# Decode attention, forward and backward: the K and V loads of the forward given to the load queue in the order in which their buffers come free

## The chip, the cores and the metric

The kernel runs on one core of a Trainium2 chip. The metric is the device time of one execution in microseconds (us), as a median of several executions. All runs told here were fast; executions of one kernel lie within about 0.5% of its median. A ratio of two kernels is the mean time of the fast runs of one over the mean of the other's in the same rounds, so it is not quite the ratio of the medians quoted.

Engines: PE is TensorE, DVE is VectorE, ACT is ScalarE, POOL is GpSimd, SP is the queue that issues the loads of K, V and the weights.

## The reference, cut to what matters

```python
def _A_ref(x, k_cache, v_cache, wq, wo):        # Sq = 1, 32 heads, Sk = 8192, Dh = 192, bf16
    q = (x @ wq) ...
    scores = einsum('bhqd,bhkd->bhqk', q, k) * Dh ** (-0.5)
    p = softmax(scores)
    o = einsum('bhqk,bhkd->bhqd', p, v)
    return o.reshape(...) @ wo
# around it: layer norms, an adaptive modulation and a small MLP.
# The result is the output and the gradients of nine inputs, among them k_cache and v_cache.
```

Each head has 3.1 MB of K and 3.1 MB of V. The forward reads both once, and along the way collects per-head matrices from K and the weighted V that spare the backward a second pass over K. The backward reads V once more and writes dK and dV.

## The kernel before

The forward is a software pipeline over heads. In the pass i of the loop, head i gets its scores (`x`), head i-1 its softmax and three of four quarters of the matmuls with K and weighted V (`y`), and head i-2 the last quarter and its output (`z`). K lies in five buffers of 1.57 MB (half a head each), V in three.

```python
NKB = 5                                       # K buffers, used in turn
vp = ctx.enter_context(tc.tile_pool(name="vp", bufs=3))   # V buffers
# ...
def load_k(h, t):
    kb = KB[(2 * h + t) % NKB]
    nc.sync.dma_start(out=kb, in_=K_hd[h][:, t * JH : (t + 1) * JH, :])
    return kb
# ...
ORDER = {mybir.EngineType.PE, mybir.EngineType.DVE, mybir.EngineType.Activation}
# ...
with tc.manual_schedule(engines=ORDER):       # these engines: as written; SP is left to the scheduler
    for i in range(HQ + 2):
        # ...
        if x is not None:
            x["k"] = [load_k(i, 0), load_k(i, 1)]
            x["v"] = [load_v(i, 0)]
            # ...
        if y is not None:
            dot_sum(y["d1"], y["S"][:, JH:J])              # DVE
            # ...
        if x is not None:
            pa = dot_mul(x["k"][0], qh)                    # DVE, first product of the head (line 264)
        # ...
        if z is not None:
            m_quarter(3, z["k"][1], ...)                   # PE; frees K buffer of (i-2, 1)
        # ... softmax of head i-1 on ACT ...
        if x is not None:
            dot_half(pa)                                   # DVE
            x["d0"] = dot_tree(pa, psR, DH // 2)           # PE, six matmuls 128x512 (line 275)
        if y is not None:
            vs0 = scale_v(0, y["v"][0], E4, Ef)            # 9 of 16 rows on DVE, 7 on ACT (line 319)
            m_quarter(0, y["k"][0], vs0, ...)
            vs1 = scale_v(1, y["v"][0], E4, Ef)            # frees V buffer of (i-1, 0)
        if x is not None:
            x["v"].append(load_v(i, 1))
        if z is not None:
            mt = m_out(...)                                # ACT, three copies from PSUM
        if last:                                           # odd i
            po = pair_sums(...)                            # PE, one-column f32 matmuls
        # ...
            m_quarter(1, y["k"][0], vs1, ...)              # frees K buffer of (i-1, 0)
        # ... second product, pair_o on DVE, third quarter, weight loads ...
        if y is not None:
            y["vs"] = scale_v(3, y["v"][1], E4, Ef)        # frees V buffer of (i-1, 1)
```

The queue's order was whatever the scheduler made of this. In the built program it repeats every two heads; with even h: V(h,1), weights, **K(h+1,0)**, K(h+1,1), V(h+1,0), K(h+2,0), V(h+1,1), K(h+2,1), V(h+2,0) (the load of the output weights moves a little).

Of the kernel before, what the change touches and what calls it, by code (L numbers as in the profile page):

```python
# [20 lines left out]
def kernel(  # L21
# [29 lines left out]
    _, HQ, S, DH = A_k_cache.shape  # L51
# [59 lines left out]
    def tcol(n, name, dtype=FP32):  # L111
        return tmp.tile([P, n], dtype, name=name)
# [67 lines left out]
    def load_w(view3, lo, hi):  # L180
        w = wst.tile([P, ND, CW], BF16, name="w_st", tag="w", bufs=1)
        nc.sync.dma_start(out=w[:, :, 0 : hi - lo], in_=view3[:, :, lo:hi])
        return w

    def load_wo(t):

        w = wst.tile([P, 3, D], BF16, name="wo_st", tag="wo")
        nc.sync.dma_start(out=w, in_=wo_v[t])
        return w
# [67 lines left out]
    def load_v(h, t):  # L257
        v = vp.tile([P, JH, DH], BF16, name="v_sb")
        nc.sync.dma_start(out=v, in_=V_hd[h][:, t * JH : (t + 1) * JH, :])
        return v  # L260

    def dot_mul(src, vec):
        prod = pp.tile([P, JH, DH], BF16, name="prod", tag="prod")
        V_.tensor_tensor(out=prod, in0=src, in1=vec[:, None, :].to_broadcast([P, JH, DH]), op=ALU.mult)  # L264
        return prod
# [12 lines left out]
    def dot_sum(ps, dst):  # L278
        V_.reduce_sum(out=dst, in_=ps, axis=AX.X)  # L279
# [5 lines left out]
    with tc.tile_pool(name="kp", bufs=1) as kp, tc.tile_pool(name="vs", bufs=3) as vsp, tc.tile_pool(name="ft", bufs=2) as ft, \  # L285
# [7 lines left out]
# [4 lines that stand above are left out]
# [9 lines left out]
        def scale_v(q, v, E4, Ef):  # L306
            vs = vsp.tile([P, JQ, VW], BF16, name="vs")
            j0 = q * JQ
            v0 = (q % 2) * JQ
            n = JQ - NVA  # L310
            A_.copy(out=vs[:, :, DH:VW], in_=E4[:, j0 : j0 + JQ, :])
            V_.tensor_tensor(  # L312
                out=vs[:, 0:n, 0:DH].rearrange("p j (a b) -> p j a b", b=4),
                in0=v[:, v0 : v0 + n, :].rearrange("p j (a b) -> p j a b", b=4),
                in1=E4[:, j0 : j0 + n, None, :].to_broadcast([P, n, DH // 4, 4]),
                op=ALU.mult,
            )
            for k in range(n, JQ):
                A_.activation(out=vs[:, k, 0:DH], in_=v[:, v0 + k, :], func=ACT.Copy, scale=Ef[:, j0 + k : j0 + k + 1])  # L319
            return vs  # L320

        def m_quarter(q, kb, vs, mp, op):
            j0 = (q % 2) * JQ
            z = q == 3
            for k in range(JQ):
                T_.matmul(mp[:, 0:MW], lhsT=kb[:, j0 + k, 0:P], rhs=vs[:, k, 0:MW], start=(q == 0 and k == 0), stop=(z and k == JQ - 1), skip_group_check=True)  # L326

            for k in range(JQ):
                p0 = 64 * (k % 2)
                T_.matmul(mp[p0 : p0 + 64, MO : MO + MW], lhsT=kb[:, j0 + k, P:DH], rhs=vs[:, k, 0:MW], start=False, stop=(z and k >= JQ - 2), skip_group_check=True)  # L330

            for k in range(JQ):
                p0 = 32 * (k % 4)
                T_.matmul(op[p0 : p0 + 32, 0:MW], lhsT=ones_bf, rhs=vs[:, k, 0:MW], start=(q == 0 and k < 4), stop=(z and k >= JQ - 4), skip_group_check=True)  # L334
# [49 lines left out]



        ORDER = {mybir.EngineType.PE, mybir.EngineType.DVE, mybir.EngineType.Activation}
        w = load_w(wq_v, 0, CW)
        for b in range(2):
            q_half(0, b, w)  # L390
        mb = MB0
        X, os_, wo_l = {}, {}, {}
        wch = None
        with tc.manual_schedule(engines=ORDER):
            for i in range(HQ + 2):
                x = X[i] = {} if i < HQ else None
                y = X.get(i - 1) if 0 < i <= HQ else None
                z = X.pop(i - 2) if i > 1 else None
                last = z is not None and i % 2 == 1
                t = (i - 3) // 2  # L400
                if x is not None:
                    x["k"] = [load_k(i, 0), load_k(i, 1)]
                    x["v"] = [load_v(i, 0)]
                    x["S"] = ft.tile([P, J], FP32, name="S_h")
                    qh = qs_bc[:, i * DH : (i + 1) * DH]
                    if i % 2 == 0:
                        wo_l[i // 2] = load_wo(i // 2)
                if y is not None:
                    dot_sum(y["d1"], y["S"][:, JH:J])
                    m1 = tcol(1, "m1")  # L410
                    V_.reduce_max(out=m1, in_=y["S"], axis=AX.X)
                if x is not None:
                    pa = dot_mul(x["k"][0], qh)
                if y is not None:
                    mx = psB.tile([P, P], FP32, name="mx", tag="b")
                    T_.matmul(mx, lhsT=m1[:, 0:1].to_broadcast([P, P]), rhs=ident_f, start=True, stop=True)
                if z is not None:
                    m_quarter(3, z["k"][1], z["vs"], z["mp"], z["op"])
                if y is not None:
                    negm = tcol(1, "negm")  # L420
                    V_.reduce_max(out=negm, in_=mx, axis=AX.X, negate=True)  # L421
                    E4, Ef = softmax(i - 1, y["S"], negm)
                if x is not None:
                    dot_half(pa)
                    x["d0"] = dot_tree(pa, psR, DH // 2)
                if y is not None:
                    y["mp"] = psM.tile([P, 512], FP32, name="mp")
                    y["op"] = psO.tile([P, 256], FP32, name="op")
                    vs0 = scale_v(0, y["v"][0], E4, Ef)
                    m_quarter(0, y["k"][0], vs0, y["mp"], y["op"])  # L430
                    vs1 = scale_v(1, y["v"][0], E4, Ef)
# [3 lines that stand above are left out]
                    mt = m_out(i - 2, z["mp"], z["op"], os_)  # L435
                if last:
                    po = pair_sums((os_.pop(i - 3), os_.pop(i - 2)))
                if i % 4 == 3 and wch is not None:
                    q_half((i + 1) // 4, 0, wch)
                if y is not None:  # L440
                    m_quarter(1, y["k"][0], vs1, y["mp"], y["op"])
                if x is not None:
                    pb = dot_mul(x["k"][1], qh)
                if z is not None:
                    m_add(i - 2, z["mp"], mt)
                if last:
                    o2 = pair_o(t, po)
                if x is not None:
                    dot_half(pb)
                    x["d1"] = dot_tree(pb, psR, DH // 2)  # L450
                if y is not None:
                    vs = scale_v(2, y["v"][1], E4, Ef)
                if last:
                    A_.copy(out=AO[:, :, 2 * t : 2 * t + 2], in_=pair_ao(o2, wo_l.pop(t)))
                    e_rows_out(t, e_rows(t))
                if i % 4 == 3 and wch is not None:
                    q_half((i + 1) // 4, 1, wch)
                    wch = None
                if i % 4 == 1 and wch is not None:
                    mod_blocks(mb, nb, wch)  # L460
                    mb += nb
                    wch = None
                if i % 4 == 2 and i + 2 < HQ:
                    wch = load_w(wq_v, ((i + 2) // 4) * CW, ((i + 2) // 4 + 1) * CW)
                if i % 4 == 0 and mb < NMB:
                    nb = min(CW // P, NMB - mb)
                    wch = load_w(wm_v, mb * P, (mb + nb) * P)
                if y is not None:
                    m_quarter(2, y["k"][1], vs, y["mp"], y["op"])
                if x is not None:  # L470
                    dot_sum(x["d0"], x["S"][:, 0:JH])
                if y is not None:
                    y["vs"] = scale_v(3, y["v"][1], E4, Ef)
            while mb < NMB:
                nb = min(CW // P, NMB - mb)
                mod_blocks(mb, nb, load_w(wm_v, mb * P, (mb + nb) * P))
                mb += nb
# [126 lines left out]
    with tc.tile_pool(name="bk1", bufs=1) as bk1, tc.tile_pool(name="ob", bufs=4) as ob, tc.tile_pool(name="bst", bufs=1) as bst:  # L604
# [149 lines left out]
        for t in range(NT):  # L754
            k = max(0, (27 * t) // 8 - 2)
# [15 lines left out]
        for h in range(HQ):  # L771
            doh = do_bc[:, h * DH : (h + 1) * DH]
            qh = qs_bc[:, h * DH : (h + 1) * DH]
            for t in range(2):
                js = slice(t * JH, (t + 1) * JH)
                v = load_v(h, t)
# [54 lines left out]
```

## Time and profile before

| | before |
|---|---|
| median (first 3 runs) | 1650.76 us |
| first product of the last head in the forward | 674.2 us after the start |
| the rest (middle, backward) | 972.7 us |
| time from head to head, heads 3 to 31 | 21.43 us on average |
| DVE's wait for K, line 264 | 102.7 us |

These are lines of the profile page of the kernel before: busy time and share by engine; 40 slices of 41 us, with PE's busy tenths, the clock granted to PE in tenths, DMA's busy tenths and the traffic; and the group of DVE's products with K (after the bar: busy time and mean; then the idle time before them, and what ended most of it).

```profile
PE 1240.7 (75%) x11811; PEld 665.2 (40%) x11811; DVE 1107.8 (67%) x1273; ACT 895.8 (54%) x1948; POOL 108.3 (7%) x193
...
PE   3778887878787878865684878887678878788764
...
PEclk7898988989898988875567655567565555555555
DMA  9988878878787878754989999999999999999988
GB/s 384 366 319 304 321 299 325 329 295 334 311 326 310 347 296 329 280 214 170 380 349 399 370 401 388 403 416 422 414 386 403 389 395 376 365 394 404 405 341 330
...
L264 DVE TENSOR_TENSOR prod<-KB,qs_bc 128x6144 bf16<-128x6144 bf16 x64 | 214.7, 3355 | 120.2 <-DMA KB<-in_A_k_cache_dram 102.7
```

The forward fills the first 17 slices. There no engine is full, not even the fullest, DMA, at a share of 0.84 and 321 GB/s, and yet the largest named wait is for K data. The next line gives the stretch from 64 to 500 us, which is all forward: start and end, length, then busy time of PE, PE weight loads, DVE, ACT, POOL, and last PE's granted clock, DMA's busy share and GB/s.

```profile
64.00:500.00 436.00, 342.65 (x4650) 258.93 (x4649) 327.08 (x306) 252.15 (x799) 5.58 (x10) 0.88 0.84 321
```

How a wait comes about is seen in one odd head, number 15. From the timeline of before (start, duration, engine, line; in brackets the idle time before it and what ended it):

```profile
314.98 0.86 PE L330 MATMUL mp<-vs,KB 128*64 128x193 bf16 x16
...
316.78 1.46 PE L275 MATMUL dot_ps<-prod,ident_bf 128*128 128x512 bf16 x6 [0.50 <-DVE prod L269]
...
321.21 0.33 SPq L259 DMA_DIRECT2D v_sb<-in_A_v_cache_dram  x1
...
321.58 0.43 SPq L182 DMA_DIRECT2D w_st<-in_A_wq_dram  x1
...
322.06 1.36 SPq L295 DMA_DIRECT2D KB<-in_A_k_cache_dram  x2
...
335.46 3.36 DVE L264 TENSOR_TENSOR prod<-KB,qs_bc 128x6144 bf16<-128x6144 bf16 x1 [7.97 <-DMA KB<-in_A_k_cache_dram]
...
340.74 2.72 PE L275 MATMUL dot_ps<-prod,ident_bf 128*128 128x512 bf16 x6 [9.54 <-DVE prod L269]
```

PE ends its last use of the K buffer at about 315.8 (the end of the group at 314.98). The load into it is issued only at 322.06, behind a V load and a weight load. Head 15's product could have started at 327.5; K is there at 335.46. Then a second cost follows: PE has stood idle for 9.54 us, and its six matmuls take 2.72 us where the group at 316.78, in the middle of the work, takes 1.46. In the stretch around them the granted clock is 0.50 (third number from the right):

```profile
336.20:346.44 10.24, 5.70 (x28) 3.58 (x29) 9.37 (x6) 6.89 (x22) 0.00 (x0) 0.50 0.87 340
```

The chain of waits through the same place (start, duration, what) shows why the V load held the queue: it waited for ACT's last scaling of the old V data.

```profile
316.19 2.43 ACT vs L319 x7
318.62 0.13 ACT vs L311
318.75 2.44 ACT vs L319 x7
321.19 0.02 issue
321.21 0.33 SPq L259
321.54 0.04 issue
321.58 0.43 SPq L182
322.02 0.04 issue
322.06 13.38 DMA KB<-in_A_k_cache_dram
335.44 0.02 issue
335.46 3.36 DVE prod L264
```

### The profile page before, as it was taken

The numbers are of one execution on the slowest core, as the hardware profiler recorded it, in microseconds if no ns is written. First come the engines' busy times: TensorE is split into PE (matmuls) and PEld (weight loads), VectorE is DVE, ScalarE is ACT, GpSimd is POOL, SyncE is SP. The second block draws the span as 40 slices with busy tenths as digits, with TensorE's granted clock in tenths as the row PEclk, the third lists the DMA queues.
The fourth block names the chain that finished last, engine by engine and source line by source line (L and its number), as shares of the span: only waits on it lengthen the run. The fifth ranks groups of instructions, "written<-read, shape, count | busy, mean of one in ns | idle before, by whom it ended". The sixth has DMA issues, their size and how long they took to land.

```text
span 1646.9 us, 28215 instructions
## 1 busy us (share of the span) xinstructions
PE 1240.7 (75%) x11811; PEld 665.2 (40%) x11811; DVE 1107.8 (67%) x1273; ACT 895.8 (54%) x1948; POOL 108.3 (7%) x193
## 2 busy tenths in 40 slices
PE   3778887878787878865684878887678878788764
PEld 1556665656565656653232332222222222222211
DVE  5777777778686868744665666767566666667563
ACT  1555656556565656642564556565456555555554
POOL 0000000000000000001010111111010101010101
PEclk7898988989898988875567655567565555555555
DMA  9988878878787878754989999999999999999988
GB/s 384 366 319 304 321 299 325 329 295 334 311 326 310 347 296 329 280 214 170 380 349 399 370 401 388 403 416 422 414 386 403 389 395 376 365 394 404 405 341 330
DMA packets 76477, 575.99 MB, mean 350 GB/s; under 512 B 7326, under 2 KB 25070, under 8 KB 35390
## 3 DMA queue, kind: packets, MB, share of 16 engines
q1 hardware_dynamic: 51530, 347.23, 54.7%
q0 software_dynamic: 24288, 226.44, 33.6%
q8 instruction: 92, 1.51, 0.4%
q10 hardware_dynamic: 532, 0.53, 0.1%
q14 instruction: 35, 0.29, 0.0%
HBM read 347.74 MB, written 226.43 MB: 349 GB/s over the span
## 4 chain that ended last, share of the span: by engine, by line
issue 35%; PE 23%; DMA 18%; DVE 12%; ACT 7%; POOL 4%; SPq 1%; POOLq 0%; ACTq 0%; DVEq 0%
DMA KB<-in_A_k_cache_dram 12%; PE dot_ps L275 7%; DVE prod L264 6%; PE mp L326 5%; ACT vs L319 4%; DVE prod L269 2%; DMA w_st<-in_w_mod_dram 2%; PE mp L330 2%; DMA out_dram<-dK 2%; DMA w_st<-in_A_wq_dram 1%; POOL out_dram L793 1%; POOL out_dram L790 1%; PE po L364 1%; ACT dV L732 1%; PE dv_ps L731 1%
## 5 line engine op out<-in xcount | busy, mean ns | idle before, releaser
L275 PE MATMUL dot_ps<-prod,ident_bf 128*128 128x512 bf16 x1152 | 480.3, 548 | 186.5 <-DVE prod L269 145.5
L732 ACT CAST dV<-dv_ps 128x768 bf16<-128x768 f32 x512 | 387.8, 809 | 206.3 <-PE dv_ps L731 191.0
L319 ACT ACTIVATE vs<-v_sb,Ef 128x192 bf16<-128x192 bf16 x896 | 323.3, 443 | 0.0
L264 DVE TENSOR_TENSOR prod<-KB,qs_bc 128x6144 bf16<-128x6144 bf16 x64 | 214.7, 3355 | 120.2 <-DMA KB<-in_A_k_cache_dram 102.7
L275 PEld LDWEIGHTS <-ident_bf 128*128 128x128 bf16 x1152 | 118.7, 117 | 374.3 <-issue 347.9
L731 PE MATMUL dv_ps<-do_bc,er_b 1*128 1x192 bf16 x2048 | 220.7, 326 | 59.0 <-ACT dV L732 58.0
L736 DVE TENSOR_TENSOR dK<-qs_bc,dS 128x6144 bf16<-128x6144 bf16 x64 | 214.2, 3346 | 10.8 <-DMA out_dram<-dK 10.7
L326 PE MATMUL mp<-vs,KB 128*128 128x193 bf16 x2048 | 219.0, 265 | 0.5 <-ACT vs L319 0.5
L264 DVE TENSOR_TENSOR prod<-v_sb,do_bc 128x6144 bf16<-128x6144 bf16 x64 | 214.3, 3348 | 3.5 <-ACT do_bc L673 3.5
L326 PEld LDWEIGHTS <-KB 128*128 128x128 bf16 x2048 | 195.4, 106 | 27.9 <-issue 14.3
L279 DVE TENSOR_REDUCE dP<-dot_ps 128x32 f32<-128x512 f32 x64 | 44.2, 691 | 238.3 <-PE dot_ps L275 238.3
L731 PEld LDWEIGHTS <-er_b 1*128 1x128 bf16 x2048 | 65.0, 102 | 295.0 <-issue 291.5
L312 DVE TENSOR_TENSOR vs<-v_sb,E 128x1728 bf16<-128x1728 bf16 x128 | 131.6, 1049 | 0.7 <-ACT E L300 0.6
L300 ACT ACTIVATE E<-S_h,negm 128x256 bf16<-128x256 f32 x32 | 16.3, 508 | 190.1 <-DVE negm L421 190.1
L269 DVE TENSOR_TENSOR prod<-prod 128x3072 bf16<-128x3072 bf16 x64 | 112.1, 1751 | 0.6
L330 PE MATMUL mp<-vs,KB 128*64 128x193 bf16 x2048 | 112.1, 253 | 0.0
L622 PE MATMUL wT_ps<-ident_bf,w_st 128*128 128x128 bf16 (+1 forms) x470 | 52.0, 290 | 68.8 <-DMA w_st<-in_w_mod_dram 26.0
L330 PEld LDWEIGHTS <-KB 128*64 128x64 bf16 x2048 | 84.3, 111 | 22.6 <-issue 22.6
L790 POOL DMA_DIRECT2D out_dram<-dV x64 | 35.4, 552 | 659.0 <-ACT dV L732 659.0
L623 ACT COPY wqT<-wT_ps 128x1024 bf16<-128x1024 bf16 (+1 forms) x52 | 50.4, 969 | 50.0 <-PE wT_ps L622 40.5
L622 PEld LDWEIGHTS <-w_st 128*128 128x128 bf16 (+1 forms) x470 | 37.7, 132 | 88.9 <-issue 47.0
L334 PE MATMUL op<-vs,ones_bf 128*32 128x193 bf16 x2048 | 66.2, 250 | 0.0
(207 smaller groups left out, 856.1 us busy)
## 6 DMA issues: line engine op xcount, KB each, us to landing
v_sb<-in_A_v_cache_dram SPq DMA_DIRECT2D x128, 1536.0 KB
KB<-in_A_k_cache_dram SPq DMA_DIRECT2D x64, 1536.0 KB
out_dram<-dV POOLq DMA_DIRECT2D x64, 1536.0 KB, 8.7
out_dram<-dK POOLq DMA_DIRECT2D x64, 1536.0 KB, 12.5
w_st<-in_A_wq_dram SPq DMA_DIRECT2D x16, 960.0 KB
wo_st<-in_A_wo_dram SPq DMA_DIRECT2D x32, 480.0 KB
out_dram<-stg POOLq DMA_DIRECT2D x13, 960.0 KB, 13.9
w_st<-in_w_mod_dram SPq DMA_DIRECT2D x8, 960.0 KB
```

The costliest lines, as they stand in the source:

```text
L264: V_.tensor_tensor(out=prod, in0=src, in1=vec[:, None, :].to_broadcast([P, JH, DH]), op=ALU.mult)
L269: V_.tensor_tensor(out=prod[:, :, 0:w], in0=prod[:, :, 0:w], in1=prod[:, :, w : 2 * w], op=ALU.add)
L275: T_.matmul(ps, lhsT=ident_bf, rhs=prod[:, :, k : k + TS], start=(k == 0), stop=(k == w - TS))
L312: V_.tensor_tensor(out=vs[:, 0:n, 0:DH].rearrange("p j (a b) -> p j a b", b=4), in0=v[:, v0 : v0 + n, :].rearrange("p j (a b) -> p j a b", ...
L319: A_.activation(out=vs[:, k, 0:DH], in_=v[:, v0 + k, :], func=ACT.Copy, scale=Ef[:, j0 + k : j0 + k + 1])
L326: T_.matmul(mp[:, 0:MW], lhsT=kb[:, j0 + k, 0:P], rhs=vs[:, k, 0:MW], start=(q == 0 and k == 0), stop=(z and k == JQ - 1), skip_group_chec ...
L330: T_.matmul(mp[p0 : p0 + 64, MO : MO + MW], lhsT=kb[:, j0 + k, P:DH], rhs=vs[:, k, 0:MW], start=False, stop=(z and k >= JQ - 2), skip_grou ...
L334: T_.matmul(op[p0 : p0 + 32, 0:MW], lhsT=ones_bf, rhs=vs[:, k, 0:MW], start=(q == 0 and k < 4), stop=(z and k >= JQ - 4), skip_group_check ...
L622: T_.transpose(out=tp[lo:hi, (x - x0) * P : (x - x0 + 1) * P], in_=src, identity=ident_bf)
L731: T_.matmul(ps[:, b, k * DH : (k + 1) * DH], lhsT=er[p0 : p0 + 1, 2 * m + k, :], rhs=doh[p0 : p0 + 1, :], start=True, stop=True)
L732: A_.copy(out=dV4[:, 2 * q : 2 * q + 2, m * PW : (m + 1) * PW], in_=ps[:, :, 0:PW])
L736: V_.tensor_tensor(out=out3[:, n0_:n1_, :].rearrange("p j (a b) -> p j a b", b=4), in0=vec.rearrange("p (a b) -> p a b", b=4)[:, None, :, ...
```

## The change

The intent is to place each load right behind the use that frees its buffer, one head ahead, and to hold the queue to that order.

```diff
-        ORDER = {mybir.EngineType.PE, mybir.EngineType.DVE, mybir.EngineType.Activation}
+        ORDER = {mybir.EngineType.PE, mybir.EngineType.DVE, mybir.EngineType.Activation, mybir.EngineType.SP}
...
-        X, os_, wo_l = {}, {}, {}
+        X, os_, wo_l = {0: {"k": [load_k(0, 0), load_k(0, 1)], "v": [load_v(0, 0)]}}, {}, {}
+        wo_l[0] = load_wo(0)
...
-                x = X[i] = {} if i < HQ else None
+                x = X.get(i)
+                nx = X[i + 1] = {"k": [], "v": []} if i + 1 < HQ else None
...
                 if x is not None:
-                    x["k"] = [load_k(i, 0), load_k(i, 1)]
-                    x["v"] = [load_v(i, 0)]
...
                     m_quarter(3, z["k"][1], z["vs"], z["mp"], z["op"])
+                if nx is not None:
+                    nx["k"].append(load_k(i + 1, 0))
...
                     m_quarter(1, y["k"][0], vs1, y["mp"], y["op"])
+                if nx is not None:
+                    nx["k"].append(load_k(i + 1, 1))
...                                    (the load of wo moves to the end of the odd head before)
                     y["vs"] = scale_v(3, y["v"][1], E4, Ef)
+                if nx is not None:
+                    nx["v"].append(load_v(i + 1, 0))
```

Nothing is computed differently. In the built programs the instruction order on PE, DVE, ACT and POOL is the same, line numbers aside. Only the load queue differs, and only in the forward. The new order, for every head: K(i+1,0), V(i,1), K(i+1,1), weights, V(i+1,0). K(h+1,0) of an odd head h+1 no longer stands behind V(h,1), and no weight load stands before it.

More of the change, by code (lines that the diff above doesn't have):

```diff
@@ L401 @@
                 if x is not None:
-                    x["k"] = [load_k(i, 0), load_k(i, 1)]
-                    x["v"] = [load_v(i, 0)]
                     x["S"] = ft.tile([P, J], FP32, name="S_h")
                     qh = qs_bc[:, i * DH : (i + 1) * DH]
-                    if i % 2 == 0:
-                        wo_l[i // 2] = load_wo(i // 2)
                 if y is not None:
@@ L462 @@
                     wch = None
+                if i % 2 == 1 and i + 1 < HQ:
+                    wo_l[(i + 1) // 2] = load_wo((i + 1) // 2)
                 if i % 4 == 2 and i + 2 < HQ:
```

## The prediction

> **What bounds the kernel now.** The slice rows split the span: forward attention from 0 to about 690 us, a short middle, then the backward with DMA at 0.9 or more. The change touches only the forward. There no engine is full: the busy table by 100 us stretches gives VectorE (DVE) 70-78%, TensorE (PE) 75-82%, DMA 79-86% at 301-332 GB/s. The chain of waits from 250 to 420 us gives its largest share, 36%, to K loads. The groups put DVE's wait for K (line 264) at 102.7 us. It falls almost only on odd heads: 7 to 8 us each, from head 13 on 7.7 and 4.7 in turn. Heads 3 to 31 advance by 21.4 us a head ((674.2-74.2)/28).
>
> **Why.** The load queue runs in one order. In the timeline the K buffer for odd head 15 came free at about 316 us, but its load was given out at 322.06, behind a V load that waited for ScalarE (ACT) until 321.2 and a weight load. Two K loads and a V load then stood together; K landed at 335.4, 8 us after DVE was ready. Between such bursts DMA had stretches at 0 GB/s.
>
> **What the change does.** No operation is added or removed. Line numbers aside, the instruction order of PE, DVE, ACT and POOL is the same in both builds; only the load queue differs, only in the forward. Each load of head i+1 now stands right after the use that frees its buffer. By an even head's timeline, K0's buffer comes free 4.7 us after the head's first product, K1's at 11.5; they are needed at about 17 and 24: 12 us for a transfer of 3.7 us at 420 GB/s.
>
> **Cost.** Without the K wait an even head took 16.0-16.7 us, which is DVE's busy time (16.2). Odd heads took 18.8-21.5, but started cold: after the wait six accumulating matmuls took 2.72 us instead of 1.46. This agrees with the Trainium skill ("TensorE: Matmul & The Clock Gate", Part 1): an idle array falls to half clock; the granted clock was 0.62 in such a stretch, 1.00 in a busy one. Warm, I estimate odd heads at 18 us. The other floor is bandwidth: a pair of heads moves 13.2-14.4 MB; with loads queued traffic ran at 410-430 GB/s, so 32-34 us a pair. Compute (about 34.5) and DMA (33) are then nearly equal; with friction, 36 us a pair, 18 a head. Almost all of the wait is on the critical path: (21.4-18.0) x 28 = 95 us, and about 8 us in the first three heads. Middle and backward keep their time.
>
> **Prediction: 1547 us, 80% range 1526 to 1582.** Faster by over 2%: 0.94; within 2%: 0.05; slower: 0.01.
>
> **What will show it.** DVE's wait for K falls from 102.7 us to under 20. Odd and even heads take 16-19 us. Forward traffic rises to about 385 GB/s, DMA share above 0.9; PE's granted clock in the forward above 0.93. The last head's first product starts near 570 us instead of 674. The backward is as long as before, within 5 us.
>
> **What would make it wrong.** Loads may not sustain 400 GB/s with buffers freed one at a time: waits on K or V remain and heads take 19-20 us (about 1590). V, now behind K, may come late and hold ACT or DVE. The odd heads' chain through the pair sums may stay at 19-20 us even when warm. Or DMA and DVE fit better than I allow: 17.2 us a head, about 1525.

## The result, and the profile after

| | before | after |
|---|---|---|
| median | 1651.26 us (1648.20 to 1653.11, 4 runs) | 1517.20 us (1510.78 to 1522.38, 4 runs) |
| ratio | 1 | 0.9188 (0.9149 to 0.9226) |
| first product of head 3 (profiled run) | 74.2 us | 64.9 us |
| first product of head 31 | 674.2 us | 543.7 us |
| rest of the span | 972.7 us | 976.9 us |
| DVE's wait for K (4.9 us of it for the first load of all, in both) | 102.7 us | 5.5 us |
| even heads, from their first product to that of the next head, mean of heads 4 to 30 | 22.72 us, of which 6.3 are the next head's wait for K | 16.28 us |
| odd heads, the same, heads 3 to 29 | 20.13 us | 17.92 us |

The direction was right, but the gain was 134 us where 104 were forecast, and the measured time lies below the range. The lines of the page of the kernel after:

```profile
PE 1209.5 (80%) x11811; PEld 645.4 (42%) x11811; DVE 1105.0 (73%) x1273; ACT 895.9 (59%) x1948; POOL 108.0 (7%) x193
...
PE   3999999998999995477668788776887788777773
...
PEclk7999999999999997566655555675555555556555
DMA  9999999999999985498989999999999999999978
GB/s 379 401 402 419 414 414 406 398 398 402 391 414 399 390 331 208 161 366 338 427 351 368 404 395 410 418 423 387 381 385 378 404 364 379 375 402 404 401 309 357
...
L264 DVE TENSOR_TENSOR prod<-KB,qs_bc 128x6144 bf16<-128x6144 bf16 x64 | 214.4, 3350 | 9.9 <-DMA KB<-in_A_k_cache_dram 5.5
```

The stretch from 64 to 500 us, as above:

```profile
64.00:500.00 436.00, 401.80 (x5836) 309.67 (x5833) 410.22 (x385) 316.07 (x1002) 7.18 (x13) 0.98 1.00 405
```

DVE now works 94% of the forward (410.2 of 436), PE's granted clock is 0.98 instead of 0.88, and DMA is shown busy all the time at 405 GB/s. The load of an odd head's first K half, of head 17, from the timeline of after:

```profile
293.80 0.86 PE L330 MATMUL mp<-vs,KB 128*64 128x193 bf16 x16
...
294.69 0.33 SPq L295 DMA_DIRECT2D KB<-in_A_k_cache_dram  x1
...
305.38 3.35 DVE L264 TENSOR_TENSOR prod<-KB,qs_bc 128x6144 bf16<-128x6144 bf16 x1
...
310.65 1.46 PE L275 MATMUL dot_ps<-prod,ident_bf 128*128 128x512 bf16 x6 [1.48 <-DVE prod L269]
```

It is issued as soon as the buffer is free (294.66), 10.7 us before the product that reads it; the product waits for nothing, and the six matmuls take 1.46 us. The chain of waits no longer passes through DMA. Through the end of odd head 17 it reads:

```profile
312.62 2.43 ACT vs L319 x7
315.04 0.20 ACT M L337
315.24 0.01 issue
315.25 0.32 ACT mt L339
315.57 0.02 issue
315.60 0.33 ACT osb L341
315.93 0.04 issue
315.97 0.69 PE po L364 x6
316.66 0.12 PE po L365 x2
316.77 0.33 PE po L366 x2
317.10 0.02 issue
317.12 0.19 DVE rz L371
```

This is ACT's scaling, ACT's copies, PE's pair sums, then DVE.

### The profile page after: what moved, and what is told of

Its sections match the earlier page's. It is cut to its first block, busy times and chain, and to the rows that moved or that the text cites. A ratio compares the mean times of both kernels' runs of the same rounds, so it can differ in the third digit from the quotient of the medians.

```text
span 1520.6 us, 28209 instructions
## 1 busy us (share of the span) xinstructions
PE 1209.5 (80%) x11811; PEld 645.4 (42%) x11811; DVE 1105.0 (73%) x1273; ACT 895.9 (59%) x1948; POOL 108.0 (7%) x193
## 4 chain that ended last, share of the span: by engine, by line
issue 33%; PE 23%; DVE 22%; ACT 10%; DMA 7%; POOL 4%; SPq 0%; POOLq 0%; ACTq 0%; DVEq 0%
DVE prod L264 11%; PE dot_ps L275 10%; ACT vs L319 5%; DVE prod L269 3%; DVE vs L312 3%; PE mp L326 3%; DMA w_st<-in_w_mod_dram 2%; PE dv_ps L737 2%; DVE S_h L279 2%; ACT dV L738 2%; PE mp L330 2%; PE wT_ps L628 2%; POOL out_dram L799 1%; POOL out_dram L796 1%; DMA w_st<-in_A_wq_dram 1%
## 5 line engine op out<-in xcount | busy, mean ns | idle before, releaser
L275 PE MATMUL dot_ps<-prod,ident_bf 128*128 128x512 bf16 x1152 | 464.9, 532 | 86.6 <-DVE prod L269 46.5
L326 PE MATMUL mp<-vs,KB 128*128 128x193 bf16 x2048 | 198.8, 250 | 0.5 <-ACT vs L319 0.5
L737 PEld LDWEIGHTS <-er_b 1*128 1x128 bf16 x2048 | 64.9, 102 | 295.7 <-issue 293.0
L326 PEld LDWEIGHTS <-KB 128*128 128x128 bf16 x2048 | 178.6, 99 | 20.6 <-issue 6.0
```

What stands on the lines that cost most here:

```text
L275: T_.matmul(ps, lhsT=ident_bf, rhs=prod[:, :, k : k + TS], start=(k == 0), stop=(k == w - TS))
L326: T_.matmul(mp[:, 0:MW], lhsT=kb[:, j0 + k, 0:P], rhs=vs[:, k, 0:MW], start=(q == 0 and k == 0), stop=(z and k == JQ - 1), skip_group_chec ...
L737: T_.matmul(ps[:, b, k * DH : (k + 1) * DH], lhsT=er[p0 : p0 + 1, 2 * m + k, :], rhs=doh[p0 : p0 + 1, :], start=True, stop=True)
```

## The experiments

Three questions were open: does the place of one load in the queue make the whole wait; where do the 33 us of gain come from that are not DVE's wait (130.5 us to the last head, less 102.7 - 5.5 = 97.2); and what sets the pace now, since the forecast had charged extra time for a nearly full DMA. A kernel with the loads placed as in the change but SP left to the scheduler was only built: the built program is the same, byte for byte, as the changed kernel's, so it was not run. Hence the moved places alone produce this order, and the fourth engine in `ORDER` does nothing more here.

### 1. The K load of odd heads put back behind the V load (`odd_late`)

```diff
-                if nx is not None:
+                if nx is not None and i % 2 == 1:
                     nx["k"].append(load_k(i + 1, 0))
...
                     x["v"].append(load_v(i, 1))
+                if nx is not None and i % 2 == 0:
+                    nx["k"].append(load_k(i + 1, 0))
```

> The changed kernel with one part undone: the first K load of each odd head stands behind the second V load of the even head before it, as in the kernel before; the weight loads stay late. Order theory (the place of this one load makes the wait): it is given out about 10 us after the even head's first product instead of 4.7, lands behind that V load, and DVE waits 3 to 5 us on each of 15 odd heads, which then start with a cold TensorE: 1590 to 1625 us, DVE's wait for K 45 to 75 us. Rival (the gain comes from the even spread of loads as a whole, and one load out of place does not matter): 1515 to 1535 us, wait for K under 15 us.

Measured: 1612.09 us (before: 1649.09), ratio 0.9776 (0.9741 to 0.9811). DVE's wait for K is 71.4 us, of which 4.9 belong to the first load of all:

```profile
L264 DVE TENSOR_TENSOR prod<-KB,qs_bc 128x6144 bf16<-128x6144 bf16 x64 | 214.7, 3355 | 88.9 <-DMA KB<-in_A_k_cache_dram 71.4
```

Every odd head from 3 on waits, 3.6 to 5.3 us. One K load in four, moved back behind one V load, costs about 95 us against the changed kernel. The rival, that the even spread as a whole does it, falls.

### 2. The weight load ahead of it as well (`odd_late_w`)

As `odd_late`, and this block moved up from the end of the head to the place just before the late `load_k(i + 1, 0)`:

```python
                if i % 4 == 2 and i + 2 < HQ:
                    wch = load_w(wq_v, ...)
                if i % 4 == 0 and mb < NMB:
                    nb = min(CW // P, NMB - mb)
                    wch = load_w(wm_v, ...)
```

> As odd_late, and the weight load again ahead of that K load, which gives nearly the load order of the kernel before, but by manual order. Order theory: the old time comes back, 1635 to 1665 us, wait for K 90 to 110 us, with 7.5 to 8 us on odd heads that have a weight load before them. Rival (some of the gain comes from the manual schedule of the queue or from the weight loads of the output projection): 1600 us or less.

Measured: 1650.79 us, ratio to before 1.0004 (0.9969 to 1.0039); wait for K 100.9 us; the last head's first product at 674.3 us. The old time is back, under manual order. From head 13 on the odd heads behind a weight load wait 7.5 to 7.8 us and the others 3.6 to 4.9, as in the kernel before. So the two places explain the whole difference: about 95 us for the V load in front, about 39 for the weight load in front of that.

### 3. Manual order alone (`manual_only`)

```diff
-        ORDER = {mybir.EngineType.PE, mybir.EngineType.DVE, mybir.EngineType.Activation}
+        ORDER = {mybir.EngineType.PE, mybir.EngineType.DVE, mybir.EngineType.Activation, mybir.EngineType.SP}
```

(in the kernel before)

> The kernel before with its load queue put under manual order and nothing moved: K0, K1 and V0 of a head stand behind V1 of the head before, for even heads too. Order theory: even heads now wait 4 to 5 us as well and start cold, so slower than before: 1690 to 1770 us, wait for K 150 us or more, on even and odd heads. Rival (manual order by itself helps): faster than 1640 us.

Measured: 1656.98 us, ratio 1.0047 (1.0013 to 1.0080); wait for K 118.2 us. The sign was right, the size was far off. In this order every head's K stands behind the V load of the head before, but an even head waits at most 4.4 us, mostly 2.3 or less, where 4 to 5 had been expected. The expectation had taken over the odd heads' wait, before which an even head of 16 us runs. Before an even head an odd one runs, which is longer: from its first product to the next head's it took 20.7 us here. That this covers most of the late load is argued from these two lengths, not tested by itself.

### 4. PE kept at work during the wait (`before_warm`)

In the kernel before, in odd heads, behind the last quarter's matmuls:

```diff
                     m_quarter(3, z["k"][1], z["vs"], z["mp"], z["op"])
+                if x is not None and i % 2 == 1 and i > 2:
+                    wps = psS.tile([P, 512], FP32, name="warm", tag="s")
+                    for k in range(36 if i % 4 == 3 or i < 12 else 24):
+                        T_.matmul(wps, lhsT=ident_bf, rhs=qs_bc[:, 0:512], start=True, stop=True)
```

> The kernel before, with 24 or 36 idle matmuls (128x512, about 0.216 us each) on TensorE in each odd head from head 3 on, at the place where it stands idle during the wait for K; nothing reads what they write. Cold theory (the part of the 130 us that is not DVE's wait for K, about 33 us, is work that ran at half clock after the wait): the wait for K stays at 90 to 110 us, the groups of six matmuls after it take 1.5 us instead of 2.72, and the time falls by 20 to 35 us, to 1615 to 1632 us. Rival (the wait for K grows by what the odd heads save, since the loads set the pace, or the 33 us come from elsewhere): within 8 us of before.

Measured: 1622.11 us, ratio 0.9840 (0.9808 to 0.9873; under 2%, but clear of 1), with DVE's wait for K nearly unchanged at 100.0 us instead of 102.7. From the timeline, head 15 again:

```profile
317.61 7.94 PE L422 MATMUL warm<-qs_bc,ident_bf 128*128 128x512 bf16 x36
...
326.56 1.45 PE L275 MATMUL dot_ps<-prod,ident_bf 128*128 128x512 bf16 x6 [1.01 <-DVE prod L269]
```

480 matmuls that compute nothing make the kernel 27 us faster. The last head's first product stands at 640.5 us instead of 674.2, which is 33.7 us; odd heads take 17.93 us, as in the changed kernel (17.92), instead of 20.13. The profiled run gives part of this back after the forward (977.9 us for the rest). Less the 2.7 us by which the wait for K is shorter, the warm array is worth about 31 us. This is the other part of the gain: of 130.5 us to the last head 97 are the wait itself and about 31 are work that ran at half clock after each wait; some 2 us are not traced to either.

### 5. The changed kernel again (`after_again`)

> The changed kernel once more, as the measure for the runs beside it. 1510 to 1524 us, ratio to before 0.916 to 0.922 under every theory.

Measured: 1518.85 us, ratio 0.9197 (0.9179 to 0.9214); head 31 at 543.9 us. This run is the measure for the three that follow, from the same chip.

### 6. Half of each K load left out (`half_k`)

```diff
-            nc.sync.dma_start(out=kb, in_=K_hd[h][:, t * JH : (t + 1) * JH, :])
+            n = JH if h < 3 else JQ
+            nc.sync.dma_start(out=kb[:, 0:n, :], in_=K_hd[h][:, t * JH : t * JH + n, :])
```

> The changed kernel with every K load from head 3 on cut to the first half of its columns (the rest of the buffer keeps the data of an earlier head: a wrong result on purpose). About 48 MB of the forward's 218 MB are not loaded. Compute theory (after the change the order of DVE, ScalarE and TensorE sets the pace, not the traffic, although DMA is shown busy all the time): within 8 us of the changed kernel, traffic falls to about 320 GB/s in the forward, heads still take 17.1 us on average. DMA theory (400 to 416 GB/s is the floor): faster by 20 us or more.

Measured: 1516.08 us, ratio 0.9184 (0.9166 to 0.9202), result wrong as intended. (By the pages, 302.1 MB are read in all instead of 347.7, so 45.6 MB are gone.) Head 31 starts at 541.9 us, 1.9 us earlier. The stretch from 64 to 500 us:

```profile
64.00:500.00 436.00, 401.76 (x5845) 309.28 (x5843) 411.75 (x386) 317.59 (x1007) 7.18 (x13) 0.99 0.84 315
```

Compare this with the two such lines above. The traffic and the DMA share are those of the kernel before (0.84, 321), the pace is that of the kernel after. DMA at share 1.00 and 405 GB/s set no pace. The friction in the forecast was for a limit that did not act.

### 7. One more row of V on ACT (`nva8`)

```diff
-    NVA = (7 * JQ) // 16
+    NVA = (8 * JQ) // 16
```

> The changed kernel with one more of each 16 scaled V rows on ScalarE and one less on DVE (8 and 8 instead of 7 and 9). DVE theory (its busy time sets the pace of all heads): 128 groups get about 0.117 us shorter on DVE, so 10 to 15 us faster. Chain theory (odd heads follow ScalarE's scaling and TensorE's pair sums, not DVE's busy time): even heads get 0.4 to 0.5 us shorter, odd heads 0.3 to 0.7 us longer, in sum within 5 us of the changed kernel. DMA theory: no change in any head.

Measured: 1538.01 us, ratio 0.9312 (0.9288 to 0.9337): 19 us slower than the changed kernel, which no theory had said. Even heads take 16.46 us instead of 16.28, odd heads 18.91 instead of 17.93. In the chain of waits ACT's scaling has 39% of the stretch from 300 to 345 us, where it has 15% in the changed kernel. DVE does less and is idle more (390 of 436 us busy instead of 410 in `after_again`). DVE's busy time alone is thus not the floor. A likely reading, not tested by itself, is that the chain from softmax through ACT's scaling to the copies and DVE's next step is about as long in every head, so that lengthening ACT lengthens even heads too. The split of 9 and 7 is near the balance from this side; 6 on ACT was not tried.

### 8. to 10. The new chain in odd heads, taken apart (`pair_late`, `mout_early`, `mout_pair`)

`pair_late` moves DVE's operations on the pair sums behind the halving of the second product:

```diff
-                if last:
-                    o2 = pair_o(t, po)
                 if x is not None:
                     dot_half(pb)
+                if last:
+                    o2 = pair_o(t, po)
+                if x is not None:
                     x["d1"] = dot_tree(pb, psR, DH // 2)
```

> The changed kernel with DVE's four small operations on the pair sums moved behind the halving of the second product, so that DVE does not wait for TensorE's pair sums. If compute sets the pace: DVE's wait for the pair sums (about 0.94 us on each odd head, 12.9 us in 14 heads) goes away, 8 to 15 us faster, odd heads 16.5 to 17 us except those where TensorE sets the pace. If DMA sets it: within 5 us of the changed kernel, with new waits for K or V.

Measured: 1517.04 us, ratio 0.9195 (0.9176 to 0.9215): no gain. The wait for the pair sums is gone, but DVE's wait for the second dot product grew from 6.2 to 12.3 us (64 to 500 us, against `after_again`), and head 31 comes only 3.4 us earlier.

`mout_early` moves ACT's copies ahead of the second quarter's scaling:

```diff
                     m_quarter(0, y["k"][0], vs0, y["mp"], y["op"])
+                if z is not None:
+                    mt = m_out(i - 2, z["mp"], z["op"], os_)
+                if y is not None:
                     vs1 = scale_v(1, y["v"][0], E4, Ef)
...
-                if z is not None:
-                    mt = m_out(i - 2, z["mp"], z["op"], os_)
```

> The changed kernel with ScalarE's three copies of the head before (M, mt, osb) moved ahead of the second quarter's scaling, behind the first's. If the odd heads follow ScalarE's scaling, these copies, TensorE's pair sums and DVE, in this order, the pair sums come about 2 us earlier, DVE's wait for them (12.9 us in 14 heads) goes away or nearly so, and the time falls by 5 to 15 us against the changed kernel (ratio to before 0.910 to 0.916). If that chain is not what holds odd heads: within 4 us, or slower because the second quarter's scaling is 0.95 us later.

Measured: 1516.07 us, ratio 0.9182 (0.9156 to 0.9207): a miss. The wait for the pair sums fell to 4.4 us (from 11.4 in `after_again`, 64 to 500 us), but 7.6 us of wait for K appeared, and head 31 stays at 543.9. A likely reason, not tested, is that V(i,1)'s buffer is now freed about 0.95 us later, with the loads behind it in the queue.

`mout_pair` has both moves.

> Both moves together: the copies early, and DVE's four small operations on the pair sums behind the halving of the second product. If both waits are links of one chain (taking one away alone makes the other end last, as the late pair operations alone moved the wait to the second dot product), odd heads come down to 16.6 to 17.2 us and the time falls by 10 to 18 us against the changed kernel (ratio to before 0.909 to 0.914). If TensorE's own order sets odd heads: within 4 us of the changed kernel.

Measured: 1513.38 us, ratio 0.9178 (0.9153 to 0.9204), and again, `mout_pair_again`:

> mout_pair once more, on the same chip, as the measure for mout_pair_warm: ratio to before 0.915 to 0.920.

1513.60 us, ratio 0.9169 (0.9156 to 0.9181). Odd heads fall to 16.45 or 17.1 us where nothing else happens, but about half of them (seven of 14, then eight) take 17.7 to 18.8. Against the changed kernel's 0.9197 the two ratios are 0.2 to 0.3% lower, from different chips, with intervals that touch: not a gain that these runs make certain. It misses the 10 us expected. With these moves the traffic is at 407 GB/s and waits for K come up again (3.2 us from 64 to 500 us here, 7.6 in `mout_early`, 0.6 in the changed kernel). Whether traffic, which set no pace in experiment 6, becomes the next limit once the chain is shorter was not tested; `half_k` with both moves would tell.

### 11. PE kept warm in the pair sums (`mout_pair_warm`)

```diff
                 T_.matmul(po[:, 4 + b : 5 + b], lhsT=c32, rhs=os2[b][:, DH:MW], start=True, stop=True)
+                if b == 0:
+                    wps = psB.tile([P, 512], FP32, name="warm", tag="b")
+                    for k in range(4):
+                        T_.matmul(wps, lhsT=ident_bf, rhs=qs_bc[:, 0:512], start=True, stop=True)
```

(in `mout_pair`)

> Both moves of mout_pair, and four idle matmuls (128x512) between the two halves of the pair sums, whose own matmuls are one column wide. In mout_pair six of 14 odd heads still took 17.7 to 18.8 us instead of 16.45 or 17.13. Cold theory (in those heads the granted clock falls during the pair sums, and the matmuls after it run at half speed): these heads come down to 16.5 to 17.5 us, the last head's first product stands near 530 us instead of 539.5, and the time is 6 to 12 us below mout_pair (ratio to before 0.909 to 0.915). If the clock falls for another cause: no change, or 1 us more on odd heads.

Measured: 1517.91 us, ratio 0.9203 (0.9188 to 0.9219), against 0.9169 for `mout_pair_again` on the same chip: slower by 0.4%. The stretches from 64 to 500 us, first of `mout_pair_again`, then of `mout_pair_warm` (third number from the right: granted clock):

```profile
64.00:500.00 436.00, 407.01 (x5894) 314.37 (x5892) 414.68 (x386) 319.96 (x1014) 7.18 (x13) 0.98 1.00 407
```

```profile
64.00:500.00 436.00, 406.31 (x5883) 308.99 (x5894) 412.87 (x386) 317.61 (x1007) 7.17 (x13) 1.00 1.00 406
```

The clock of `mout_pair_again` in odd head 7: PE is shown busy through the whole of the first stretch, which ends with the pair sums, and the clock is halved in the second.

```profile
139.77:143.18 3.41, 3.41 (x55) 3.00 (x54) 3.35 (x3) 2.59 (x9) 0.00 (x0) 1.00 1.05 427
143.18:146.60 3.42, 3.42 (x19) 2.50 (x18) 3.38 (x8) 1.78 (x6) 0.00 (x0) 0.50 1.01 420
```

It is halved like this in six of the 14 odd heads there (17.8 to 18.8 us). With the four matmuls the clock stays at 1.00, and five of these six are 0.6 to 0.8 us shorter although each now holds the four matmuls (about 0.9 us), so it was the clock that made them long. (The sixth, number 23, has waits for K in this run and takes 18.56; number 9, with 18.81, is long in both runs without a low clock.) But the four matmuls now stand in every odd head, and the other twelve take 17.2 or 18.0 us: odd heads average 17.75 instead of 17.69. The remedy costs what it saves.

## Why the prediction was wrong

- **What bounds the kernel: right.** The wait of odd heads for K, made by the place of their first K load, was the limit. `odd_late_w` brings it back by that place and the weight load's alone.
- **The wait on the critical path: right.** It fell by 97 us, from 102.7 to 5.5 (forecast: under 20), and none of it came back elsewhere in the forward.
- **The cold PE: right in kind and in size.** Warm odd heads were estimated at 18 us and took 17.92; even heads at 16.0 to 16.7 and took 16.28. `before_warm` measures this part alone at about 31 us up to the last head (33.7 less 2.7 of shorter waits).
- **The friction: this step failed.** The prediction put it as "Compute (about 34.5) and DMA (33) are then nearly equal; with friction, 36 us a pair, 18 a head". Measured were 17.10 us a head, 34.2 a pair. The added 1.5 us a pair are 21 us over 14 pairs; the rest of the miss inside the forward is 34.5 against 34.2 (4 us) and the first three heads (9.3 us against 8). The friction had been reasoned from DMA's busy share and from an estimate of its limit at 410 to 430 GB/s; no trace had shown two nearly equal floors adding up. `half_k` shows that with 45.6 MB less the last head starts 1.9 us earlier, so DMA added nothing like 21 us. The pace was that of compute, 34.2 us a pair. The traffic in the forward was 405 GB/s, above the 385 that I expected.
- **The middle and the backward: right.** 972.7 against 976.9 us in the profiled run, 973.3 when repeated.
- **The range.** The case "17.2 us a head, about 1525" was named as what would make the prediction wrong, but set outside the range's lower end. It should have been the middle: the wait had been measured (102.7 us), the cold matmuls too, at least in one group (2.72 instead of 1.46 us), and the term that was added had no measurement behind it.
- **What sets the pace now** is not one engine's busy time alone. DVE works 94% of the time, but one row less for it and one more for ACT made the kernel 19 us slower, and breaking single links of the odd heads' chain moved the wait to another link. Which mix of these orders would be fastest stays open.

## What to carry to other kernels

A load queue works in order, so read what each load waits for before it is issued: a load whose buffer is free behind one whose buffer is not is a hidden wait, and it costs what the work before it does not cover. Count the second cost of a wait too, the work that runs at half clock after it; here it was a quarter of the gain. Do not add friction for a resource because its busy share nears one: take some of its work away and look at whether anything moves.

## What the Trainium skill lacked or had wrong

- "TensorE: Matmul & The Clock Gate", Part 1, says that an idle array falls to half clock and warms up with activity. The trace agrees: six matmuls took 2.72 us after 9.54 us of idle time and 1.46 us otherwise. What it lacks is that an array shown busy can fall too: right after PE's one-column f32 pair sums the granted clock fell to 0.50 for 3.4 us (in `mout_pair_again` after PE was shown busy for 3.41 of 3.41 us; in the changed kernel in four of the 14 odd heads, which took 19.0 to 19.1 us), and four 128x512 matmuls between the sums held it at 1.00 (`mout_pair_warm`). Whether the single column or the f32 type does it was not taken apart.
- "Perfetto Trace Analysis", section "Identifying the Most-Contended Engine", says that the occupancy of the 16 DMA engines misleads, to use HBM utilization instead, and then to find which DMA resource binds. The first part holds: share 1.00 (changed kernel) and 0.84 (`half_k`) gave the same time. Utilization alone was not enough here either: 405 GB/s and 315 GB/s gave the same time, while 321 GB/s in the kernel before went with a 130 us longer forward.
- "DMA: Bandwidth & Descriptors", section "Where 436 GB/s comes from", says that for transfers between HBM and SBUF the HBM side binds at about 358 GB/s a core. A single core sustained 405 GB/s over 436 us here; the same page's section "Bandwidth" does note that its numbers above that are for one core with its neighbour idle.
- "DMA: Bandwidth & Descriptors", section "Anatomy of one DMA — SWDGE (gpsimd) path", says that any semaphore wait happens on the issuing sequencer, before the DMA is dispatched. The loads of this case are issued from SP, and the trace agrees for them too: the V load waits until ACT is done at 321.19 and is issued at 321.21. What this page does not spell out is the consequence for the order of loads: all loads behind the waiting one wait with it. Here one K load behind one V load, in every second head, cost about 95 us of 1612 (`odd_late` against the changed kernel).
